# Ten and four extra products on TensorE around the state's part of two pieces, in a kernel of a chunked scan and two dense layers

## The chip, the core and the metric

The kernel runs on one core of a Trainium2 chip. That core has five engines that work side by side and wait for each other through semaphores: PE (TensorE, the matrix products, with PEld for its weight loads), DVE (VectorE), ACT (ScalarE), POOL (GpSimd) and SP (SyncE, which here only issues transfers). Each engine takes its own instructions in a fixed order. The metric is the time of one execution of the whole program, in microseconds of device time; the median of several runs counts.

## The reference, cut to what matters

```python
log_a = np.log(np.clip(a, 1e-06, 1.0))
for c in range(nc):                                  # 24 chunks of 32 steps
    cum = np.cumsum(la, axis=-1)
    M = np.einsum('bhin,bhjn->bhij', Cc, Bc) * np.exp(cum_i - cum_j) * causal
    y[:, :, sl] = M @ xc + (Cc @ state) * np.exp(cum)
    state = decay_full * state + sum_j(Bc_j xc_j * decay_from_j)
x = y.transpose(0, 2, 1, 3).reshape(3072, 256)
g = lrelu(x @ w_in)            # 256 -> 2048, slope 0.01
x = g @ w_out                  # 2048 -> 256
h = relu(x @ w2_in)            # 256 -> 2048
out = (h * h) @ w2_out         # 2048 -> 256
```

A scan over 4 sequences of 768 steps (8 heads, head size 32, state size 16) gives 3072 rows of 256 numbers. Two dense layers follow, each 256 to 2048 to 256, with a leaky relu in the first and a squared relu in the second. All of it is wanted in fp32.

## The kernel before, in words

**Tiling.** The 3072 rows are cut into 12 *pieces* of 256 steps (TP), three to a sequence. The scan of a piece (scan_piece, L300) writes the piece's rows as a pair yh and yl (L389, L390): an upper part that TensorE can take as fp32r, and the rest. The pieces are gathered into 8 *blocks*: the first four blocks are one piece each, the last four two pieces each. A block goes through layer 1 and then through layer 2. The constant ORDER (L39) says in which order: "10 11 12 20 ..." is layer 1 of blocks 0, 1 and 2, then layer 2 of block 0, and so on. I write "block 11" for layer 1 of block 1, as ORDER does; blocks 10, 11 and 12 need pieces 0, 1 and 2.

**A layer of a block.** The 2048 middle columns are 16 tiles of 128. For a block of one piece two tiles make a *group*, so a layer has eight groups. A group has 12 first products (hmm, L417 to L419, into a PSUM tile hp of the pool ph, which has three buffers under one tag "h"), its activation (act: gh and t on ACT, gl on DVE at L433), and 12 second products (omm: eight with gh at L445 and L446, four with gl at L450), which add up over all groups in two PSUM tiles o0 and o1. When the last group is in, finish (L452) copies o out: upper part on ACT (L458), lower part yl on DVE (L459). Each of o0 and o1 has one buffer only, so the next layer's second products wait for these copies.

**A piece's scan.** TensorE has three short bursts: 32 products S (L340, L341), 48 products Y (L365 to L367), and at the end 32 products that add the earlier state's part to Y (L385, L386). Between the last two lies the state's chain: the scan stt on DVE (L212), its split in two parts shl (ACT L374, DVE L376), the transpose t16 on DVE (L378), four transfers into the block-diagonal operand sbd (L310), and the 32 products; then ACT writes yh (L389) and DVE yl (L390), and the block's first hmm can start.

**Weights.** They arrive as 64-bit words and are taken apart in the kernel: load_w issues the transfer, split_w (ACT L129, L132), split_w1 (DVE L140, L141) and split_w2 (ACT L152, DVE L153) make an upper and a lower part of each of the 32 chunks. All of it happens in the first 150 us, beside the scans.

**What sets the order.** The code emits scan steps, weight steps and groups interleaved; a scheduler then fixes the order of each engine's instructions before the program runs. On the chip an engine does not leave that order: what stands behind a waiting instruction waits too.

Of the kernel before, what the change touches and what calls it, by code (L numbers as in the profile page):

```python
# [8 lines left out]
F32 = mybir.dt.float32  # L9
# [9 lines left out]
P = 128  # L19
# [18 lines left out]

ORDER = "10 11 12 20 13 21 14 22 23 15 24 16 25 17 26 27"  # L39
LAG = {1: 2, 2: 3}  # L40
W_AHEAD = 4


@with_exitstack
def ssd_moe_kernel(ctx: ExitStack, tc: tile.TileContext, in1, in2, w1i, w1o, w2i, w2o, out):
# [6 lines left out]
    nc = tc.nc  # L52
# [7 lines left out]
    ph = ctx.enter_context(tc.tile_pool(name="ph", bufs=3, space=bass.MemoryType.PSUM))  # L60
# [14 lines left out]
    xbh = cp.tile([P, U, 4, T], F16, name="xbh")  # L75
# [14 lines left out]
    w_hi, w_lo = {}, {}  # L90
# [19 lines left out]
    def load_w():  # L110
        nm, c = wq.pop(0)
        if nm == "2o" and c >= 5:
            st = yp.tile([P, 2, 256], I64, tag="y2", name="wst")
        else:
            st = wp.tile([P, 2, 256], I64, tag="w", name="wst")
        if nm[1] == "i":
            sl = (slice(None), slice(None), slice(c * 256, c * 256 + 256))
        else:
            sl = (slice(None), slice(2 * c, 2 * c + 2), slice(None))
        nc.sync.dma_start(st, w_dram[nm][sl])  # L120
        w_loaded.append((nm, c, sl, st))
# [50 lines left out]
    def load_piece(p):  # L172
        v = sp.tile([P, U * (N + T + D)], F32, tag="in1", name="in1")
        w = sp.tile([P, U * 2 * T], F32, tag="in2", name="in2")
        nc.sync.dma_start(v, in1[p])
        nc.sync.dma_start(w, in2[p])
        return part(v, N + T, D), part(v, 0, N), part(w, T, T), part(v, N, T), part(w, 0, T), part(w, 0, T + N)
# [38 lines left out]
    def in_chunks(v):  # L216
        return v.rearrange("p k (c t) -> p (k c) t", t=T)
# [59 lines left out]
    def powers(mx):  # L277
# [19 lines left out]
        nc.vector.tensor_tensor(sbp, sc[:, 2:3], pm, ALU.mult)  # L297
        return sc, isc, sbp

    def scan_piece(p, tiles, get_y):  # L300
        x_t, b_t, bt_t, ct_t, az, mk = tiles
        if p < NPC:
# [60 lines left out]
        for u in range(U):  # L363
            o = Y[:, u, 0 : T + N]
# [8 lines left out]
        shl = sp.tile([P, HG, NC, 2, N], F16, tag="xh", name="shl")  # L373
        nc.scalar.copy(shl[:, :, :, 0, :], sv)  # L374
        yield
        nc.vector.tensor_tensor(shl[:, :, :, 1, :], sv, shl[:, :, :, 0, :], ALU.subtract)  # L376
        t16 = sp.tile([P, U, D], F16, tag="xl", name="t16")
        nc.vector.transpose(t16.rearrange(fl), shl.rearrange("p g c k n -> p (g c k n)"))  # L378
        yield
# [3 lines left out]
        for u in range(U):  # L383
            o = Y[:, u, 0:T]
            nc.tensor.matmul(o, sbd[:, u], qh[:, u], start=False, stop=False, skip_group_check=True)  # L385
            nc.tensor.matmul(o, sbd[:, u], ql[:, u], start=False, stop=True, skip_group_check=True)  # L386
        yield
        yh, yl = (in_chunks(v) for v in get_y())
        nc.scalar.activation(yh, Y[:, :, 0:T], AF.Copy, scale=fac)  # L389
        nc.vector.scalar_tensor_tensor(yl, Y[:, :, 0:T], fac, yh.bitcast(F32), ALU.mult, ALU.subtract)  # L390


# [96 lines left out]
    loaded = {0: load_piece(0)}  # L489
    for _ in range(W_AHEAD):  # L490
        load_w()

    def scans():
        for p in range(NP):
            bd = sequence_scales(p // NPC + 1) if p % NPC == NPC - 1 and p + 1 < NP else iter(())
            for i, _ in enumerate(scan_piece(p, loaded.pop(p), piece_y(p))):
                if i == QN[p] - 7 and p + 1 < NP:
                    loaded[p + 1] = load_piece(p + 1)
                next(bd, None)
                yield p  # L500
            for _ in bd:
                pass
            yield p
# [29 lines left out]
    def second(lag):  # L533
        while len(pend) > lag:
            ph_, ms = pend.pop(0)
            ph_.omm(ms)
            if ms[-1] == KO - 1:
                ph_.finish()
# [3 lines left out]
    for layer, i in order:  # L542
        p0, n = blocks[i]
        yh, yl = ys.pop(i) if layer == 2 else ys[i]
        ph_ = Phase(layer, p0, n, yh, yl)
        for m in range(0, KO, 2 // n):
# [7 lines left out]
            pend.append((ph_, ms))  # L554
            second(LAG[n])
            acc += 1.0 if len(wq) > 18 else 0.4
# [55 lines left out]
```

## Time and profile before

| | |
|---|---|
| median of 3 runs | 652.35 us (650.02 to 653.43) |
| the profiled execution | 649.59 us |
| its span, first to last instruction | 647.8 us |
| PE busy in the span | 592.5 us, 91% |
| DVE busy in the span | 420.4 us, 65% |
| ACT busy in the span | 356.9 us, 55% |
| mean granted TensorE clock | 0.989 |

The busy shares are means over stages with different limits. "Granted clock" is the share of TensorE's full clock: 1.00 is 2.4 GHz, 0.50 is 1.2 GHz, and anything between is a mix of the two within the stretch that is shown. An instruction's listed duration is longer than the step to the next one of its kind, because instructions overlap at their ends; what a row of instructions costs is the distance between their starts.

### The profile page before, as it was taken

How to read it: one execution, taken by the hardware profiler on the slowest of the kernel's cores; microseconds unless marked ns; L12 is line 12 of the kernel's file. 1: busy time of each engine (PE TensorE's matmuls, PEld its weight loads, DVE VectorE, ACT ScalarE, POOL GpSimd, SP SyncE). 2: the span in 40 equal slices, each digit the busy share in tenths (PEclk: the TensorE clock that was granted, in tenths of full speed). 3: DMA queues.
4: the chain of work that ended last, by engine and by line, in shares of the span. 5: the costliest groups of instructions: out<-in, count | busy, mean ns of one | idle time of the engine just before them, and what ended most of it. 6: DMA issues, size and time to landing. Idle time of an engine off the chain costs nothing.

```text
span 647.8 us, 11305 instructions
## 1 busy us (share of the span) xinstructions
PE 592.5 (91%) x4440; PEld 514.8 (79%) x4440; DVE 420.4 (65%) x726; ACT 356.9 (55%) x630; POOL 5.1 (1%) x14
## 2 busy tenths in 40 slices
PE   0278695999999999999999999999999999999997
PEld 0177595999999988899987888888888888788885
DVE  7989999898768854576554586563565322554553
ACT  5999776665555545545535555455544433544442
POOL 3000000000000000000000000000000000000000
PEclk9999898899999999999999999999999999999999
DMA  9775765423635422202212212212000000000000
GB/s 323 240 242 136 238 138 150 127 61 65 172 33 149 76 73 24 50 34 42 50 50 25 50 33 25 50 66 25 8 1 10 33 0 1 0 1 2 32 2 32
DMA packets 111397, 46.48 MB, mean 72 GB/s; under 512 B 94320, under 2 KB 101104, under 8 KB 111344
## 3 DMA queue, kind: packets, MB, share of 16 engines
q1 hardware_dynamic: 111344, 45.76, 27.2%
q8 instruction: 35, 0.57, 0.4%
q14 instruction: 18, 0.15, 0.1%
HBM read 36.83 MB, written 3.15 MB: 62 GB/s over the span
## 4 chain that ended last, share of the span: by engine, by line
PE 72%; DVE 16%; ACT 4%; DMA 4%; issue 3%; SPq 0%; DVEq 0%; ACTq 0%
PE o L445 12%; PE hp L417 12%; PE hp L419 12%; PE hp L418 11%; PE o L446 11%; PE o L450 11%; DMA all<-in 3%; DVE gl L433 2%; DVE wst L140 2%; DVE wst L141 2%; DVE t L431 1%; DVE mx L266 1%; DVE e L194 1%; DVE lt L188 1%; DVE wl1i L153 1%
## 5 line engine op out<-in xcount | busy, mean ns | idle before, releaser
L433 DVE TENSOR_TENSOR gl<-t,gh 128x512 fp32r<-128x512 f32 x192 | 132.0, 688 | 130.1 <-ACT t L428 80.4
L427 ACT ACTIVATE gh<-hp 128x512 fp32r<-128x512 f32 x96 | 57.2, 596 | 95.4 <-PE o L446 77.8
L432 ACT CAST gh<-t 128x512 fp32r<-128x512 f32 x96 | 59.6, 621 | 74.8 <-DVE t L431 64.5
L417 PE MATMUL hp<-yl,wh1i 128*128 128x256 f32 (+1 forms) x256 | 89.4, 349 | 9.5 <-DVE yl L390 9.5
L431 DVE TENSOR_TENSOR t<-t 128x512 f32<-128x512 f32 x96 | 66.1, 688 | 44.5 <-ACT t L430 44.4
L418 PE MATMUL hp<-yh,wh1i 128*128 128x256 f32 (+1 forms) x256 | 88.8, 347 | 0.0
L419 PE MATMUL hp<-yh,wl1i 128*128 128x256 f32 (+1 forms) x256 | 88.8, 347 | 0.0
L430 ACT ACTIVATE t<-hp 128x512 f32<-128x512 f32 x96 | 57.3, 597 | 57.2 <-PE hp L419 54.6
L445 PE MATMUL o<-gh,wl1o 128*128 128x256 f32 (+1 forms) x256 | 84.8, 347 | 3.6 <-DVE wl1o L153 3.4
L417 PE MATMUL hp<-yl,wh2i 128*128 128x256 f32 (+1 forms) x256 | 86.8, 339 | 0.0
L419 PE MATMUL hp<-yh,wl2i 128*128 128x256 f32 (+1 forms) x256 | 86.5, 338 | 0.0
L418 PE MATMUL hp<-yh,wh2i 128*128 128x256 f32 (+1 forms) x256 | 86.2, 337 | 0.0
L445 PE MATMUL o<-gh,w2o 128*128 128x256 f32 (+1 forms) x256 | 83.6, 343 | 2.1 <-DVE yl L459 1.9
L446 PE MATMUL o<-gh,wh1o 128*128 128x256 f32 (+1 forms) x256 | 82.8, 339 | 0.0
L446 PE MATMUL o<-gh,w2o 128*128 128x256 f32 (+1 forms) x256 | 81.7, 336 | 0.0
L417 PEld LDWEIGHTS hp<-yl,wh1i 128*128 128x128 f32 x256 | 50.7, 198 | 15.1 <-issue 5.8
L450 PE MATMUL o<-gl,wh1o 128*128 128x256 f32 (+1 forms) x256 | 61.1, 339 | 0.6 <-DVE gl L433 0.6
L450 PE MATMUL o<-gl,w2o 128*128 128x256 f32 (+1 forms) x256 | 60.8, 337 | 0.0
L445 PEld LDWEIGHTS o<-gh,wl1o 128*128 128x128 f32 x256 | 48.2, 188 | 12.0 <-DVE wl1o L153 5.8
L428 ACT ACTIVATE t<-hp 128x512 f32<-128x512 f32 x96 | 56.9, 593 | 0.0
L419 PEld LDWEIGHTS hp<-yh,wl1i 128*128 128x128 f32 x256 | 50.6, 198 | 5.9 <-issue 0.2
L418 PEld LDWEIGHTS hp<-yh,wh1i 128*128 128x128 f32 x256 | 50.8, 198 | 5.4
(124 smaller groups left out, 982.1 us busy)
## 6 DMA issues: line engine op xcount, KB each, us to landing
in<-in SPq DMA_DIRECT2D x12, 640.0 KB, 4.5
in<-in SPq DMA_DIRECT2D x12, 512.0 KB, 3.3
all<-in SPq DMA_DIRECT2D x15, 384.0 KB, 3.7
wst<-w1i SPq DMA_DIRECT2D x8, 512.0 KB, 9.2
wst<-w1o SPq DMA_DIRECT2D x8, 512.0 KB, 4.6
wst<-w2o SPq DMA_DIRECT2D x8, 512.0 KB, 5.7
wst<-w2i SPq DMA_DIRECT2D x8, 512.0 KB, 5.0
out_t<-ob SPq DMA_DIRECT2D x8, 256.0 KB, 2.2
```

The source lines that it names most:

```text
L417: nc.tensor.matmul(hp, wh, self.xl[:, :, k], start=(k == 0), stop=False)
L418: nc.tensor.matmul(hp, wh, self.xh[:, :, k], start=False, stop=False)
L419: nc.tensor.matmul(hp, wl, self.xh[:, :, k], start=False, stop=(k == KI - 1))
L427: nc.scalar.activation(gh, hp, AF.Lrelu)
L428: nc.scalar.activation(t, hp, AF.Lrelu)
L430: nc.scalar.activation(t, hp, AF.Relu)
L431: nc.vector.tensor_tensor(t, t, t, ALU.mult)
L432: nc.scalar.copy(gh, t)
L433: nc.vector.tensor_tensor(gl, t, gh.bitcast(F32), ALU.subtract)
L445: nc.tensor.matmul(self.o[d], wl, gh, start=(m == 0), stop=False)
L446: nc.tensor.matmul(self.o[d], wh, gh, start=False, stop=False)
L450: nc.tensor.matmul(self.o[d], wh, gl, start=False, stop=(m == KO - 1))
```

## The change

A helper warm(a, b, n) takes a PSUM tile of the pool ph under the tag "h", the same three buffers that hold hp, and runs n products of 512 columns into it. Nobody reads that tile. It is called twice in the scan of pieces 1 and 2: ten products right after DVE has written the lower part of shl (their moving operand is shl, their stationary operand the first slice of xbh), and four products right after ACT has written yh (moving operand yh, stationary operand the first weights of layer 1). Nothing else is edited. Line numbers move by up to 12.

```diff
--- before.py
+++ after.py
@@ -38,6 +38,7 @@
 
 ORDER = "10 11 12 20 13 21 14 22 23 15 24 16 25 17 26 27"
 LAG = {1: 2, 2: 3}
+WARM = (1, 2)
 W_AHEAD = 4
 
 
@@ -297,6 +298,12 @@
         nc.vector.tensor_tensor(sbp, sc[:, 2:3], pm, ALU.mult)
         return sc, isc, sbp
 
+    def warm(a, b, n):
+
+        o = ph.tile([P, 512], F32, tag="h", name="warm")
+        for _ in range(n):
+            nc.tensor.matmul(o, a, b, start=True, stop=True)
+
     def scan_piece(p, tiles, get_y):
         x_t, b_t, bt_t, ct_t, az, mk = tiles
         if p < NPC:
@@ -374,6 +381,8 @@
         nc.scalar.copy(shl[:, :, :, 0, :], sv)
         yield
         nc.vector.tensor_tensor(shl[:, :, :, 1, :], sv, shl[:, :, :, 0, :], ALU.subtract)
+        if p in WARM:
+            warm(xbh[:, 0].rearrange("p h t -> p (h t)"), shl.rearrange("p g c k n -> p (g c k n)"), 10)
         t16 = sp.tile([P, U, D], F16, tag="xl", name="t16")
         nc.vector.transpose(t16.rearrange(fl), shl.rearrange("p g c k n -> p (g c k n)"))
         yield
@@ -385,8 +394,11 @@
             nc.tensor.matmul(o, sbd[:, u], qh[:, u], start=False, stop=False, skip_group_check=True)
             nc.tensor.matmul(o, sbd[:, u], ql[:, u], start=False, stop=True, skip_group_check=True)
         yield
-        yh, yl = (in_chunks(v) for v in get_y())
+        ya = get_y()
+        yh, yl = (in_chunks(v) for v in ya)
         nc.scalar.activation(yh, Y[:, :, 0:T], AF.Copy, scale=fac)
+        if p in WARM:
+            warm(w_hi["1i"][:, 0, 0:P], ya[0].rearrange("p k t -> p (k t)"), 4)
         nc.vector.scalar_tensor_tensor(yl, Y[:, :, 0:T], fac, yh.bitcast(F32), ALU.mult, ALU.subtract)
```

The scheduler orders the whole program anew. DVE's order is the same as before up to its row 127, and the same again for its last 305 rows; PE's is the same for its first 325 rows and its last 4306. In between the rows are reordered. Three places are shown.

PE, the third piece (piece 2): the end of the state's products (Y from sbd) and what follows. hp_1464 is the first group of block 12, which reads piece 2's yl_1401 and yh_1400. Before:

```order
L385 MATMUL Y_1233<-qh_1185,sbd_96 128x32
L386 LDWEIGHTS sbd_96
L386 MATMUL Y_1233<-ql_1186,sbd_96 128x32
L417 MATMUL hp_1464<-yl_1401,wh1i_110 128x256
L418 MATMUL hp_1464<-yh_1400,wh1i_110 128x256
L419 MATMUL hp_1464<-yh_1400,wl1i_111 128x256
L417 MATMUL hp_1464<-yl_1401,wh1i_110 128x256
L418 MATMUL hp_1464<-yh_1400,wh1i_110 128x256
```

In the changed kernel piece 2's pair is called yl_1428 and yh_1427, and yl_338 and yh_337 is the pair of the two blocks before:

```order
L395 MATMUL Y_1249<-ql_1202,sbd_96 128x32
L305 MATMUL warm_1430<-yh_1427,wh1i_110 128x512 x4
L429 MATMUL hp_1456<-yl_338,wh1i_110 128x256
L430 MATMUL hp_1456<-yh_337,wh1i_110 128x256
L431 MATMUL hp_1456<-yh_337,wl1i_111 128x256
L429 MATMUL hp_1456<-yl_338,wh1i_110 128x256
L430 MATMUL hp_1456<-yh_337,wh1i_110 128x256
L431 MATMUL hp_1456<-yh_337,wl1i_111 128x256
L429 MATMUL hp_1456<-yl_338,wh1i_110 128x256
L430 MATMUL hp_1456<-yh_337,wh1i_110 128x256
L431 MATMUL hp_1456<-yh_337,wl1i_111 128x256
L429 MATMUL hp_1456<-yl_338,wh1i_110 128x256
```

The four extra products wait for yh_1427, and the last group of block 11 (12 first products, hp_1456) now stands behind them; its 12 second products come later still. Before, all of block 11 stood ahead of the state's products. At the second piece it is alike: the last group of block 10 stands behind the four products, and the last but one behind the ten.

DVE, the stretch that ends with the third piece's yl (yl_1401). yl_338 from o0_1148 and o1_1149 is the finish of block 11. Before:

```order
L153 TENSOR_TENSOR wl2i_115<-wst_812,wh2i_114 128x2x256
L459 TENSOR_TENSOR yl_338<-o0_1148,yh_337 128x256
L459 TENSOR_TENSOR yl_338<-o1_1149,yh_337 128x256
L140 SCALAR_TENSOR_TENSOR wst_885<-wst_885 128x512
L194 SCALAR_TENSOR_TENSOR e1_1567<-in2_1286,d1e_97 128x512
L141 SCALAR_TENSOR_TENSOR wst_885<-wst_885 128x512
L342 TENSOR_TENSOR e1_1567<-in1_1285,e1_1567 128x512
L333 SCALAR_TENSOR_TENSOR xl_1603<-in1_1285,sc_1190,xh_1490 128x512
L153 TENSOR_TENSOR wl2i_115<-wst_885,wh2i_114 128x2x256
L140 SCALAR_TENSOR_TENSOR wst_940<-wst_940 128x512
L323 SCALAR_TENSOR_TENSOR kmx_1483<-in2_1286,sc_1190,him_1443 128x512
L390 SCALAR_TENSOR_TENSOR yl_1401<-Y_1233,fac_984,yh_1400 128x512
```

In the changed kernel piece 2's lower part, yl_1428, stands two rows above the first of these; yl_338 from o0_1164 and o1_1165 is the finish of block 11:

```order
L154 TENSOR_TENSOR wl2i_115<-wst_1087,wh2i_114 128x2x256
L141 SCALAR_TENSOR_TENSOR wst_1323<-wst_1323 128x512
L141 SCALAR_TENSOR_TENSOR wst_1454<-wst_1454 128x512
L142 SCALAR_TENSOR_TENSOR wst_1323<-wst_1323 128x512
L445 TENSOR_TENSOR gl_1471<-t_1469,gh_1470 128x512
L142 SCALAR_TENSOR_TENSOR wst_1454<-wst_1454 128x512
L445 TENSOR_TENSOR gl_1511<-t_1509,gh_1510 128x512
L154 TENSOR_TENSOR w2o_1900<-wst_1323,w2o_1900 128x512
L367 SCALAR_TENSOR_TENSOR ql_1788<-e1_1599,sc_1206,qh_1787 128x512
L445 TENSOR_TENSOR gl_1551<-t_1549,gh_1550 128x512
L471 TENSOR_TENSOR yl_338<-o0_1164,yh_337 128x256
L471 TENSOR_TENSOR yl_338<-o1_1165,yh_337 128x256
```

The finish of block 11 moved from ahead of piece 2's yl to 12 rows behind it, and weight steps (wst, wl2i) that stood behind yl now stand ahead of it.

DVE, the finish of block 12 (yl_1401 from o0_1570 and o1_1571), which is followed by layer 2 of block 0. Before:

```order
L141 SCALAR_TENSOR_TENSOR wst_1917<-wst_1917 128x512
L459 TENSOR_TENSOR yl_1401<-o0_1570,yh_1400 128x256
L433 TENSOR_TENSOR gl_1934<-t_1932,gh_1933 128x512
L459 TENSOR_TENSOR yl_1401<-o1_1571,yh_1400 128x256
L153 TENSOR_TENSOR w2o_2199<-wst_1917,w2o_2199 128x512
L431 TENSOR_TENSOR t_1981<-t_1981 128x512
L194 SCALAR_TENSOR_TENSOR e1_2272<-in2_1942,d1e_97 128x512
L333 SCALAR_TENSOR_TENSOR xl_2306<-in1_1941,sc_1190,xh_2238 128x512
L433 TENSOR_TENSOR gl_1983<-t_1981,gh_1982 128x512
L431 TENSOR_TENSOR t_2024<-t_2024 128x512
L342 TENSOR_TENSOR e1_2272<-in1_1941,e1_2272 128x512
L266 TENSOR_REDUCE mx_2661<-all_2662 128x1
```

In the changed kernel (yl_1428 from o0_1602 and o1_1603):

```order
L141 SCALAR_TENSOR_TENSOR wst_1949<-wst_1949 128x512
L383 TENSOR_TENSOR shl_2020<-stt_1971,shl_2020 128x16x16
L142 SCALAR_TENSOR_TENSOR wst_1949<-wst_1949 128x512
L387 STREAM_TRANSPOSE t16_2064<-shl_2020 128x512
L443 TENSOR_TENSOR t_1922<-t_1922 128x512
L154 TENSOR_TENSOR w2o_2231<-wst_1949,w2o_2231 128x512
L349 TENSOR_TENSOR e1_2304<-in1_1973,e1_2304 128x512
L445 TENSOR_TENSOR gl_1924<-t_1922,gh_1923 128x512
L267 TENSOR_REDUCE mx_2693<-all_2711 128x1
L443 TENSOR_TENSOR t_1964<-t_1964 128x512
L471 TENSOR_TENSOR yl_1428<-o0_1602,yh_1427 128x256
L471 TENSOR_TENSOR yl_1428<-o1_1603,yh_1427 128x256
```

The row e1<-in1 and a reduction mx<-all, which stood behind the finish, stand ahead of it now, and so do the scan e1 and another mx<-all, a few rows above the piece shown.

## Rows read from the trace of the kernel before

**Rows 1.** The page's head.

```profile
span 647.8 us, 11305 instructions
```

**Rows 2.** Stretches: length, busy us (instructions) of each engine, granted clock, DMA.

```profile
core 0: us, PE busy (x) PEld busy (x) DVE busy (x) ACT busy (x) POOL busy (x), PEclk, DMA share, GB/s
60.00:147.00 87.00, 70.35 (x747) 67.44 (x745) 83.39 (x162) 62.32 (x116) 0.00 (x0) 0.92 0.54 151
75.00:85.00 10.00, 8.40 (x58) 8.31 (x58) 9.73 (x28) 8.93 (x18) 0.00 (x0) 0.83 0.71 224
105.00:110.00 5.00, 1.11 (x34) 0.89 (x32) 5.00 (x8) 3.29 (x8) 0.00 (x0) 0.84 0.44 46
115.00:120.00 5.00, 5.00 (x31) 5.00 (x30) 3.61 (x8) 2.44 (x5) 0.00 (x0) 0.64 0.51 60
147.00:648.00 501.00, 494.90 (x3396) 422.22 (x3396) 282.51 (x445) 243.40 (x427) 0.00 (x0) 1.00 0.18 39
```

**Rows 3.** PE in order of time, second piece: start, length, engine, line, operation.

```profile
76.78 0.39 PE L417 MATMUL hp<-yl,wh1i 128*128 128x256 f32 x1 [1.60 <-DVE yl L390]
...
77.77 0.42 PE L418 MATMUL hp<-yh,wh1i 128*128 128x256 f32 x1
...
80.97 0.33 PE L418 MATMUL hp<-yh,wh1i 128*128 128x256 f32 x1
81.14 0.28 PE L419 MATMUL hp<-yh,wl1i 128*128 128x256 f32 x1
81.26 0.27 PE L417 MATMUL hp<-yl,wh1i 128*128 128x256 f32 x1
```

**Rows 4.** PE in order of time, third piece; in brackets the idle time before.

```profile
107.60 0.18 PE L385 MATMUL Y<-qh,sbd 128*128 128x32 f16 x1 [2.46 <-DMA sbd<-t]
...
114.29 0.55 PE L417 MATMUL hp<-yl,wh1i 128*128 128x256 f32 x1 [5.72 <-DVE yl L390]
114.64 0.42 PE L418 MATMUL hp<-yh,wh1i 128*128 128x256 f32 x1
...
118.48 0.35 PE L418 MATMUL hp<-yh,wh1i 128*128 128x256 f32 x1
```

**Rows 5.** ACT and DVE in order of time, ahead of the third piece's first products.

```profile
111.33 0.67 ACT L389 ACTIVATE yh<-Y,fac 128x512 fp32r<-128x512 f32 x1
112.73 0.75 DVE L323 SCALAR_TENSOR_TENSOR kmx<-in,sc,him 128x512 f16<-128x512 f32 x1
113.40 0.74 DVE L390 SCALAR_TENSOR_TENSOR yl<-Y,fac,yh 128x512 fp32r<-128x512 f32 x1
```

**Rows 6.** DVE's waits, 60 to 147 us: in total, times, longest.

```profile
DVE gl L433 <- ACT t L428: 1.8, 3, 1.4
DVE mx L266 <- DMA all<-in: 1.0, 2, 0.7
```

**Rows 7.** DVE in order of time: distances between starts.

```profile
62.28 0.69 DVE L140 SCALAR_TENSOR_TENSOR wst<-wst 128x512 int32<-128x512 int32 x1
62.88 0.69 DVE L433 TENSOR_TENSOR gl<-t,gh 128x512 fp32r<-128x512 f32 x1
...
78.64 1.22 DVE L194 TENSOR_TENSOR_SCAN e<-in,d1e 128x512 f32<-128x512 f32 x1
79.78 0.93 DVE L266 TENSOR_REDUCE mx<-all 128x1 f32<-128x768 f32 x1
80.62 0.14 DVE L243 TENSOR_SCALAR er<-rb 128x1 int32<-128x1 int32 x1
...
107.06 0.74 DVE L459 TENSOR_TENSOR yl<-o,yh 128x256 fp32r<-128x256 f32 x2
```

**Rows 8.** All engines in order of time, where block 12 ends and layer 2 begins.

```profile
146.57 0.41 DVE L459 TENSOR_TENSOR yl<-o,yh 128x256 fp32r<-128x256 f32 x1
...
147.04 0.39 PE L445 MATMUL o<-gh,w2o 128*128 128x256 f32 x1 [1.30 <-DVE yl L459]
...
147.50 0.41 DVE L459 TENSOR_TENSOR yl<-o,yh 128x256 fp32r<-128x256 f32 x1
```

**Rows 9.** PE's waits, 148 to 648 us: in total, times, longest.

```profile
PE Y L385 <- DMA sbd<-t: 0.7, 1, 0.7
PE o L445 <- DVE yl L459: 0.6, 1, 0.6
PE S L286 <- DVE dg L284: 0.3, 1, 0.3
```

## The prediction

> **What bounds the kernel now.** I read the page's head first [rows 1]: the span is 647.8 us, and the profiled execution took 649.59, so 1.8 us lie around it. The median of the runs shown is 652.35, 2.76 us more; I make the sum against 649.59 and add 2.76 at the end.
>
> Then I read the busy times by stage [rows 2], because the page's 91% for PE is a mean over two different stages. From 147 us on PE is busy 494.90 of 501 us at the full clock: there the end is set by how much PE still has to do, and a microsecond lost ahead of it is a microsecond at the end. From 60 to 147 us it is otherwise: DVE is busy 83.39 of 87 us, PE 70.35. Whether PE's gaps in that stage can close depends on what stands in DVE's queue.
>
> Then PE's rows around the two pieces. At the second piece the first products wait 1.60 us for yl and start at full clock, one every 0.12 us; from the start at 77.77 to that at 80.97 there are 15 steps of 0.213 us, and from 81.14 on 0.12 again [rows 3]. At the third piece PE waits 2.46 us for the transfers into sbd, runs the 32 products, and then stands idle for 5.72 us until DVE has written yl [rows 4]; the granted clock falls to half meanwhile (0.84 over 105 to 110 us, 0.64 over 115 to 120) [rows 2], and from 114.64 to 118.48 there are 18 steps of 0.213 [rows 4]. These slow stretches are what the extra products can act on.
>
> Last, the two releasers. yh is done at 112.00, but yl starts only at 113.40, right behind kmx: DVE has no gap there, it comes to yl when its queue does [rows 5]. And at 147.04, where layer 2 of block 0 begins its second products, PE has waited 1.30 us for the finish of block 12 on DVE [rows 8]. So DVE's queue sets both points at which PE waits longest.
>
> **The change, part by part.**
>
> *The clock.* If it stays full, 15 steps shrink from 0.213 to 0.12 at the second piece: 15 x 0.094 = 1.4 us, with the two steps at the ends 1.5. At the third piece 18 x 0.094 = 1.7, with the first and last step 1.9. Together 3.4 us of PE time; the lower bound is nothing, if the clock falls all the same.
>
> *The products themselves.* No row shows one of 512 columns in this stage. Two steps of 256 columns at full clock make 0.24 us [rows 3], at half clock 0.43. Ten cost 2.4 (4.3) us and four 0.95 (1.7) for each piece. The ten wait for DVE's lower part of shl, and the groups behind them wait as well; the cover is the idle time that followed in any case (2.46 us and 5.72 us [rows 4]). The four lie between yh and yl: yh at 112.00 plus 0.95 is 112.95, and PE was idle until 114.29. So none of the 28 lies on the path, as long as yl comes no earlier. Uncovered, all 28 would cost 6.7 us.
>
> *The group that moved behind the four products.* At the third piece PE has 24 more products to do after yh than before, the last group of block 11. Its 12 first products (1.4 us) take 112.95 to 114.4, which is when yl was ready. Its 12 second products, 1.4 us, are new work behind yl. Against the 1.9 us of the clock that leaves PE 0.5 us ahead. At the second piece the same happens, but PE's 5.72 us of idle time at the third swallow whatever it brings there.
>
> *A wait that gets longer.* The 32 products with sbd now stand on PE behind the second products of block 11's seventh group, whose gl (gl_1391) DVE does ten rows after the transpose. By DVE's steps (below) that is 6 us after it, near 110 us, and puts these products at about 110.2 instead of 107.60. yh follows near 111.9. DVE comes to yl at 113.4, so 1.5 us of cover is left and the cost is nothing; without the cover it would be what exceeds 1.5.
>
> *DVE's queue, the term that decides.* I counted the rows ahead of two points, before and after, and priced each by the distance between starts [rows 7]: 0.60 for a weight step, gl or a plain 512-column operation, 1.14 for the scan e1, 0.84 for a reduction mx<-all, 0.37 for one copy yl<-o. Ahead of the third piece's yl there are three wst rows and one wl2i more (+2.4), one gl (-0.6) and two copies (-0.74) fewer: +1.1 us. Ahead of the finish of block 12 there are one scan e1 (+1.14), one plain row e1<-in1 (+0.6), one w2o row (+0.6) and two reductions (+1.68) more: +4.0 us. That is the upper bound of how much later DVE comes to this finish, for which PE already waits [rows 8].
>
> The lower bound is set by DVE's idle time, which can fill up: 87 less 83.39, so 3.6 us from 60 to 147 [rows 2], of which 1.8 is gl waiting for ACT behind block 12's slow first products and 1.0 the reductions waiting for their transfers [rows 6]. If all of it closes, DVE comes 0.4 us later. I take the gl waits as closed (a whole group more of gl work is at hand, and block 12's products come fast) and most of the waits of the reductions: 2.5 of 3.6, nearer the full recovery, since the rows on which those waits rest move apart. That leaves +1.5 us at 147.04. PE itself would be there 0.5 us earlier than before, so it waits longer, and it is DVE's 1.5 us that pass on.
>
> *Behind it.* From 148 us on PE has 1.6 us of waits left: 0.7 for sbd, 0.6 for a finish, 0.3 for dg [rows 9]. The chains behind the first and the last do not hang on PE, so part of them closes when PE is late; I take 0.5, between nothing and 1.0.
>
> The sum: +1.5 - 0.5 = +1.0 us, so 650.6 against the profile's 649.59, and **653.4 us** beside the median of 652.35. That is 0.16%; about 0.5%, or 3.3 us, is what a measurement of this kernel can tell from no change.
>
> The Trainium skill (page "Perfetto Trace Analysis", sections "Identifying the Most-Contended Engine" and "Optimization Strategy") says to work on the engine with the highest occupancy, and that this engine may be another one in each regime of a kernel. Taken over the whole page, the rule names PE (91%) and would give the clock's 3.4 us in full; taken over 60 to 147 us, it names DVE and gives the sum above. The row of the stage is the nearer one, and I follow it.
>
> **The rivals.**
>
> *The clock's gain passes through.* If PE, not DVE, sets the time through the stage, all 3.4 us arrive: 652.35 - 3.4 = 649.0. For it speaks that over 115 to 120 us PE is busy all the time and DVE only 3.61 of 5 us [rows 2]. Against it, that at both ends of this stretch it waited for DVE, and that DVE has more to do in front of both. It decides if DVE comes to block 12's finish no later than before, that is if it recovers over 4.0 us where it has 3.6 to recover. Chance 0.12. The Trainium skill (page "TensorE: Matmul & The Clock Gate", section "Why this matters for your kernels") advises to leave no idle gaps between bursts of products, so that the full clock lasts. By that alone the time would be this rival's; the rows on the clock agree with the rule, those on DVE say that its gain has no way to the end.
>
> *DVE recovers nothing.* The second reduction that moved ahead of block 12's finish needs a transfer that can only be issued when the first one is read. If DVE waits there as it did before for such transfers (0.7 us at the longest [rows 6]), or its other waits only move, the whole +4.0 arrives and nothing closes behind: 656.4. It decides if DVE's idle time between 60 and 147 us is still 3.6 us or more. For it speaks that some 240 rows of DVE's order are new, so that a wait that closes at one row can open at another. Chance 0.17.
>
> *The change doesn't do what it says.* The clock falls at the third piece all the same: ahead of the four products PE still has idle time, before and after the 32 small products. The four then take 1.7 us to 113.7 and the 12 first products 2.6 to 116.3; the slow stretch, as long as before, ends at about 116.2. PE is then 2.0 us late for block 12 less 1.9 for starting it at full clock, and with the group's second products 1.5 us late. It had 1.30 us to wait at 147.04 [rows 8] and now has DVE's 1.5 us more: the time is the same 653.4, with at most 0.5 on top. Chance 0.23.
>
> **How the numbers follow.** My own sum has 0.48. The prediction is 653.4. Within 0.5% of 652.35 lie 0.45 of my sum's 0.48, 0.20 of the fallen clock's 0.23, 0.05 of the first rival's 0.12 (649.0 is just at the bound) and 0.06 of the second's 0.17: 0.76. Faster by over 0.5%: 0.07 from the first rival and 0.02 from the two sums: 0.09. Slower: 0.11 from the second and 0.04 from the two sums: 0.15. The range goes from 649.5, which leaves out most of the first rival, to 656.5, the upper bound of DVE's term; below it lie some 0.09, above it some 0.09.
>
> **What would show it.** The clock: granted clock of 1.00 over 75 to 85 us and about 115 to 120, steps of 0.12 us in block 12's first products. The cover: no idle time of PE closed by the extra products alone, and yl of the third piece within 1.5 us of 114.1. DVE: idle time of about 1 us from 60 to 147 in place of 3.6. The finish of block 12: PE's wait for yl L459 (L471 then) at least as long as 1.30 us, its end near 148.5. From there to the end the distance should be that of before, 500.8 us (647.8 less 147.04), shorter by no more than 1.0.
>
> I am wrong if PE waits for nothing near 147 us: then something else than DVE set the pace, and the time is lower. And I am wrong if DVE meets a new wait of over 2 us, on a transfer or on PE's reordered groups, ahead of block 12's finish: then it is higher.

## The result, and the profile after

The changed kernel takes **654.75 us** (median of 8 runs, 653.73 to 656.60) beside 651.83 us for the kernel before (8 runs, 649.72 to 653.43): ratio 1.006, 95% interval 1.0044 to 1.0075. The medians lie 2.9 us apart; the ratio, which is not that of the medians, stands for 3.9 us. Forecast were 653.4 beside 652.35, which is 1.0 us slower. The time lies in the range, the sign is right, and the loss is three to four times the forecast one.

The profiled execution of the change took 656.38 us, with a span of 654.6. Its stretches, columns as in [rows 2]:

```profile
60.00:147.00 87.00, 75.39 (x786) 69.45 (x786) 84.40 (x162) 62.70 (x113) 0.00 (x0) 1.00 0.56 154
75.00:85.00 10.00, 8.25 (x62) 7.79 (x63) 8.53 (x21) 6.64 (x12) 0.00 (x0) 1.00 0.90 298
105.00:110.00 5.00, 3.74 (x22) 2.44 (x21) 5.00 (x10) 3.19 (x7) 0.00 (x0) 1.00 0.62 139
115.00:120.00 5.00, 4.70 (x35) 4.52 (x36) 5.00 (x9) 3.34 (x7) 0.00 (x0) 1.00 0.38 39
147.00:655.00 508.00, 499.21 (x3412) 426.53 (x3410) 282.35 (x446) 244.57 (x431) 0.00 (x0) 0.99 0.18 38
```

The granted clock is 1.00 where it was 0.83, 0.84 and 0.64, and over 60 to 147 us 1.00 in place of 0.92. But it is 0.99 behind 147 us, where it was 1.00. PE around the two pieces, in order of time, answering to [rows 3, 4]:

```profile
75.74 1.19 PE L305 MATMUL warm<-yh,wh1i 128*128 128x512 f32 x4 [0.34 <-ACT yh L399]
76.76 0.28 PE L429 MATMUL hp<-yl,wh1i 128*128 128x256 f32 x1
76.89 0.28 PE L430 MATMUL hp<-yh,wh1i 128*128 128x256 f32 x1
...
105.50 2.32 PE L305 MATMUL warm<-shl,xbh 128*128 128x512 f16 x10 [1.69 <-DVE shl L383]
107.47 0.47 PE L429 MATMUL hp<-yl,wh1i 128*128 128x256 f32 x1
...
112.40 0.73 PE L462 MATMUL o<-gl,wh1o 128*128 128x256 f32 x4 [1.13 <-DVE gl L445]
112.97 0.19 PE L394 MATMUL Y<-qh,sbd 128*128 128x32 f16 x1
...
115.30 1.20 PE L305 MATMUL warm<-yh,wh1i 128*128 128x512 f32 x4 [1.36 <-ACT yh L399]
116.34 0.28 PE L429 MATMUL hp<-yl,wh1i 128*128 128x256 f32 x1
116.46 0.27 PE L430 MATMUL hp<-yh,wh1i 128*128 128x256 f32 x1
```

All first products of 256 columns run one every 0.12 us; the 15 and 18 steps of 0.213 us are gone. The idle 5.72 us of [rows 4] is gone too. What came in its place stands where block 12 ends and layer 2 begins (DVE's finish and PE's first o with w2o, answering to [rows 8]), and right behind it:

```profile
150.06 0.76 DVE L471 TENSOR_TENSOR yl<-o,yh 128x256 fp32r<-128x256 f32 x2
...
150.55 0.39 PE L457 MATMUL o<-gh,w2o 128*128 128x256 f32 x1 [1.69 <-DVE yl L471]
...
151.58 0.41 PE L458 MATMUL o<-gh,w2o 128*128 128x256 f32 x1
151.80 1.05 PE L462 MATMUL o<-gl,w2o 128*128 128x256 f32 x4
152.65 0.41 PE L429 MATMUL hp<-yl,wh2i 128*128 128x256 f32 x1
152.86 0.41 PE L430 MATMUL hp<-yh,wh2i 128*128 128x256 f32 x1
...
154.78 0.37 PE L430 MATMUL hp<-yh,wh2i 128*128 128x256 f32 x1
154.99 0.28 PE L431 MATMUL hp<-yh,wl2i 128*128 128x256 f32 x1
155.11 0.29 PE L457 MATMUL o<-gh,w2o 128*128 128x256 f32 x1
```

PE waits 1.69 us where it waited 1.30, and 1.0 us after the wait its products take 0.213 us each again, until 154.99. PE's waits behind 147 us (in total, times, longest) were 0.7, 0.6 and 0.3 in [rows 9] behind the one at 147.04; now there is, besides the 1.7 just shown, one for the state's transfers, and another slow stretch follows it:

```profile
PE Y L394 <- DMA sbd<-t: 2.5, 1, 2.5
PE o L457 <- DVE yl L471: 1.7, 1, 1.7
```

Read alone, this pair of profiles says: 3.5 us lost up to block 12's finish, 3.3 behind it. It is 6.8 us apart where the medians are 2.9 apart, so I profiled both kernels once more before reading on.

### The profile page after: what moved, and what is told of

Same layout as the page of the kernel before. It is cut to its first block, busy times and chain, and to the rows that moved or that the text cites. A ratio compares the mean times of both kernels' runs of the same rounds, so it can differ in the third digit from the quotient of the medians.

```text
span 654.6 us, 11368 instructions
## 1 busy us (share of the span) xinstructions
PE 599.8 (92%) x4468; PEld 519.0 (79%) x4468; DVE 420.3 (64%) x726; ACT 357.6 (55%) x630; POOL 5.1 (1%) x14
## 4 chain that ended last, share of the span: by engine, by line
PE 79%; DVE 13%; ACT 3%; DMA 3%; issue 2%; SPq 0%; DVEq 0%; ACTq 0%
PE o L457 13%; PE hp L429 12%; PE o L462 12%; PE hp L431 12%; PE hp L430 12%; PE o L458 12%; DVE wst L142 2%; DMA in<-in 1%; DVE gl L445 1%; DVE wst L141 1%; DVE e L195 1%; DVE lt L189 1%; DMA all<-in 1%; DVE wl1i L154 1%; PE Y L394 1%
## 5 line engine op out<-in xcount | busy, mean ns | idle before, releaser
L457 PEld LDWEIGHTS o<-gh,w2o 128*128 128x128 f32 x256 | 48.0, 188 | 8.3 <-DVE yl L471 2.1
```

The costliest lines, as they stand in the source:

```text
L457: nc.tensor.matmul(self.o[d], wl, gh, start=(m == 0), stop=False)
```

## Experiments

**Both kernels a second time** (no edit).

Kernel before: 

> The kernel before, profiled once more. In the first piece, which the change leaves alone, the 0.213 us steps of block 10's first products end at 40.0 us in the profile of before and at 42.3 in that of the change. If this end differs from one execution to the next, it lies elsewhere here, and block 12's finish (147.04 us) moves with it, by 1 to 2 us. If it is fixed by the program, it is at 40.0 again and the finish at 147.0.

The change: 

> The changed kernel, profiled once more. If the end of the first piece's slow steps differs from one execution to the next, the clock behind 147 us does as well: the slow stretches at 151.6 and 193.1 us are then gone or elsewhere, and the span is 1 to 3 us under 654.6. If they belong to the changed order, both are there again, and so is the wait of 2.5 us for the transfers into sbd near 192 us.

Measured: 652.53 and 652.17 us; the *slower* one of these two is the kernel before. The four profiles side by side ("finish" is the start of PE's first o<-gh,w2o; the second column is where the first piece's steps of 0.213 us end, which this change does not touch):

| | first piece's slow steps end | finish | finish to end of span |
|---|---|---|---|
| before, 1st profile | 40.0 | 147.04 | 500.8 |
| before, 2nd | 42.5 | 149.66 | 501.1 |
| change, 1st | 42.3 | 150.55 | 504.0 |
| change, 2nd | 40.0 | 148.16 | 502.2 |

So part of what the first pair showed was the executions', not the change's. I call an execution early when these steps end at about 40 us, and late when they end at about 42.5. DVE waits for S of that piece (row m<-S: 0.8 us in the early executions, 1.8 in the late ones). That makes 1.0 of the 2.6 us between the two finishes of the kernel before. Most of the rest enters at one reduction, which waits longer for its transfer in the late execution; the kernel before, early and late:

```profile
84.22 0.95 DVE L266 TENSOR_REDUCE mx<-all 128x1 f32<-128x768 f32 x1 [0.27 <-DMA all<-in]
87.37 0.95 DVE L266 TENSOR_REDUCE mx<-all 128x1 f32<-128x768 f32 x1 [1.71 <-DMA all<-in]
```

The change waits at such a reduction for 1.23 us in its late execution (79.49) and not at all in its early one (76.94). Whether the longer wait follows from the first piece's delay is not shown. Early beside early and late beside late, the finish comes 1.1 and 0.9 us later with the change, and the way from there to the end is 1.5 and 2.9 us longer: means 1.0 and 2.2, in sum 3.2 beside the medians' 2.9. The stretches of the second profiles, before above, the change below:

```profile
60.00:147.00 87.00, 70.42 (x738) 67.49 (x738) 82.03 (x159) 61.87 (x114) 0.00 (x0) 0.90 0.55 150
147.00:160.00 13.00, 11.70 (x122) 11.41 (x121) 11.17 (x18) 7.56 (x15) 0.00 (x0) 1.00 0.35 55
```

```profile
60.00:147.00 87.00, 76.96 (x799) 71.01 (x798) 85.69 (x164) 63.66 (x116) 0.00 (x0) 1.00 0.56 154
147.00:160.00 13.00, 11.84 (x110) 11.77 (x111) 8.31 (x14) 5.36 (x9) 0.00 (x0) 0.87 0.38 63
```

DVE's idle time from 60 to 147 us is 3.6 and 5.0 us before, 2.6 and 1.3 with the change: 2.3 us are recovered. And the clock falls behind the finish in both profiles of the change (0.87 over 147 to 160 us; the first profile's row reads the same 0.87) and in neither of before (1.00). The second slow stretch, near 193 us, is in the first profile only.

One limit holds for all that follows: the scheduler orders each edited kernel anew. I give the number of DVE's 726 rows that would have to move to make two orders equal (names without buffer numbers, so it is a lower bound). Between the kernel before and the change it is 62; change and order alone, 35; ten alone and the ten's place, 66; the two lighter kernels, 58 of 694; before and first piece alone, 3; change and the change with the next gap filled, none. Only there does an edit add products and change nothing else.

**The order without the products.**

```diff
-        for _ in range(n):
-            nc.tensor.matmul(o, a, b, start=True, stop=True)
+        nc.tensor.matmul(o[:, 0:32], a, b[:, 0:32], start=True, stop=True)
```

> Each call of the helper here makes one product of 32 columns instead of ten or four of 512: the tile is allocated and the order of all engines is nearly that of the change (the last groups stand behind the extra products, DVE has the same rows ahead of block 12's finish), but nothing fills PE's gaps. Theory A (the order costs time, by DVE's 2 to 4 us more of work ahead of block 12's finish): as slow as the change, ratio to before 1.004 to 1.008, with the clock falling at both pieces as before. Theory B (the products themselves cost, the order does not): like before, ratio 0.998 to 1.002. Theory C (the products' full clock is worth its 3.4 us, and the order costs more than the change shows): slower than the change, ratio 1.009 to 1.012.

Measured: ratio 1.0031 (1.0017 to 1.0044), 2.1 us slower. An order of this kind costs time without the products. The ratio lies between the ranges of A (from 1.004) and B (to 1.002), and its interval touches both; C, by which this kernel had to be slower than the change, falls. Beside the change's 2.9 us (3.9 by the ratio), the 28 products, with all they do for the clock, come out at +0.9 us (1.9) and not at a gain. The early profiles show two sides of that. The finish is at 150.12 in an early execution (40.2), 3.1 us later than in the early one of before and 2.0 later than in that of the change (148.16): up to the finish the products earn. Behind it this kernel needs 500.3 us and the change 502.2: there it is lost again.

**The products without a turn among hp's buffers.**

```diff
-        o = ph.tile([P, 512], F32, tag="h", name="warm")
+        o = pz.tile([P, U, T], F32, tag="S", name="warm").rearrange(fl)
```

> The extra products write a tile of the pool pz under the tag S instead of one of the three buffers that hold hp. So they take no turn among the groups, and PE's groups stand where they stood before: 96 and 192 first products ahead of the state's products of the second and third piece, none moved behind the four. By the prices of the rows DVE has 2.4 us more ahead of block 12's finish than before (the change: the same). Theory A (DVE's work ahead of that finish decides): ratio 1.002 to 1.006. Theory C (PE's clock decides once the groups stay): ratio 0.995 to 0.998. If the turn among hp's buffers is the whole cost: 0.998 to 1.002.

Measured: ratio 1.0037 (1.0023 to 1.0050). All groups stand ahead of the state's products again, and it is still 2.1 us slower: a loss of this size does not need the moved groups. The size agrees with A. The clock is not held at the third piece here (0.56 over 115 to 120 us), though all 28 products run.

**The ten alone, the four alone** (the other call is left out).

Ten alone: 

> Only the ten products behind shl, none behind yh. No group moves behind the state's products, and DVE has 0.3 us more than before ahead of block 12's finish. Theory A (order): like before, ratio 0.998 to 1.002. Theory B (the products cost): ten products at 0.24 us on two pieces, up to 4.8 us in part uncovered, ratio 1.002 to 1.007. The clock should still fall in the gap ahead of the third piece's yl, since nothing fills it.

Four alone: 

> Only the four products behind yh, none behind shl. The last group of blocks 10 and 11 moves behind them as in the change, and DVE has 1.6 us more than before ahead of block 12's finish. Theory A (order): ratio 1.002 to 1.005, most of the change's loss. Theory B (the products cost, and the ten are most of them): ratio 0.998 to 1.002.

Measured: ten alone 1.0068 (1.0048 to 1.0087), four alone 1.0003 (0.9990 to 1.0016). Both are against A: by the prices of DVE's rows the four should have cost most and the ten nothing. The ten cost 4.5 us when alone, in B's range.

**The ten's place with one small product** (the edit of the order alone, made to the kernel with the ten alone).

> As the kernel with the ten products alone (ratio 1.0068), but each of its two calls makes one product of 32 columns: the tile keeps its turn among hp's three buffers, and by the prices of the rows DVE has 0.6 us less than before ahead of block 12's finish. Theory G (the tile's turn, and the order that follows from it, cost the most): ratio 1.003 to 1.006. Theory H (the ten products' own 2.3 us on PE at each piece cost the most): ratio 0.998 to 1.002.

Measured: **0.9969** (0.9954 to 0.9983), 1.9 us *faster* than before. Against the ten alone that is 6.4 us for ten real products at two pieces, more than the 2 x 1.97 us from their first start to that of the next product (105.50 to 107.47 above). The tile's turn does not cost by itself, so G falls; the time lies even below H's range (from 0.998). That the products make the whole 6.4 us is not shown, because 66 of DVE's rows stand elsewhere in the two kernels.

**Less work for DVE.** The second of DVE's two operations on each 64-bit weight word is left out, from the kernel before and from the change; some bits of the weights are then missing.

```diff
-        nc.vector.scalar_tensor_tensor(w0, w1, -(1 << 31), w0, ALU.bitwise_and, ALU.bitwise_or)
```

Before, lighter: 

> The kernel before without the second of DVE's two operations on each 64-bit word of the weights (some bits of the weights are then missing from the output's products): by the prices of the rows DVE has 17 us less to do ahead of block 12's finish. Theory A (DVE is the bound up to 147 us): faster than before by 5 to 12 us, ratio 0.981 to 0.992. If DVE is not the bound there: 0.996 to 1.000.

Change, lighter: 

> The change without the same operation of DVE. Theory A (the full clock is worth 3.4 us of PE, and DVE's queue hides it): with DVE's queue shorter the change pays, 1 to 3.4 us less than the lighter kernel before, a quotient of the two ratios of 0.995 to 0.998. Theory D (the ten products push the work behind them back on PE, whatever DVE has to do): 1 to 4 us more, a quotient of 1.002 to 1.006.

Measured: 0.9871 (0.9845 to 0.9897) and 0.9909 (0.9881 to 0.9936): 643.08 and 645.20 us. DVE does bound the stage, since less of it takes 7.6 us off the kernel before. But with DVE busy only 74.2 and 74.3 of the 87 us, the change still costs 2.1 us. The clock was held better in five of the six executions of the lighter change (0.994 to 0.996 over the span, against 0.987), though not in the one profiled (0.988). That DVE's queue *hides a gain* of the clock has no support here: with the queue shorter no gain appears. The time is the one D expected. The lighter kernels are ordered anew as well, so the 2.1 us can't be put to one row, nor to the products alone.

**The next gap filled as well.** Four more products, into the tile of layer 2's third group, ahead of that group's own:

```diff
+FILL_M, FILL_N = 4, 4
...
+            if self.layer == 2 and self.t0 == 0 and ms[0] == FILL_M:
+                for _ in range(FILL_N):
+                    nc.tensor.matmul(self.h, w_hi["2i"][:, 0, 0:P], self.xh.rearrange("p a k t -> p (a k t)"), start=True, stop=True)
```

> The change, with four more unread products of 512 columns on PE just ahead of the first products of layer 2 of block 0's third group, that is in the place where PE waits for block 12's finish (1.68 and 1.69 us in the two profiles of the change); DVE's and PE's order is otherwise that of the change. They need no wait and take 0.95 us of the idle time. Theory E (behind 147 us the change loses 1.0 to 1.6 us because the clock falls after this wait): no steps of 0.213 us between 148 and 156 us, ratio to before 1.002 to 1.005. Rival (the clock falls there for another reason, or its fall costs nothing in the end): ratio 1.005 to 1.008 as the change, or the slow steps are still there.

Measured: 1.0039 (1.0023 to 1.0055), 1.4 us better than the change's 1.0060 by the middle values; the intervals overlap. PE around the finish, in order of time:

```profile
148.51 1.09 PE L427 MATMUL hp<-yh,wh2i 128*128 128x512 f32 x4
149.45 0.28 PE L433 MATMUL hp<-yl,wh2i 128*128 128x256 f32 x1
...
151.77 0.39 PE L461 MATMUL o<-gh,w2o 128*128 128x256 f32 x1 [0.74 <-DVE yl L475]
...
152.92 0.64 PE L466 MATMUL o<-gl,w2o 128*128 128x256 f32 x4
153.40 0.28 PE L433 MATMUL hp<-yl,wh2i 128*128 128x256 f32 x1
```

The wait is 0.74 us and the steps behind it are 0.12: the four hold the clock there, as E says. This profile has a slow stretch further on, behind a wait of 1.99 us at 191.4 (granted clock 0.79 over 190 to 198 us). One execution of this kernel had a mean granted clock of 1.000 over its span and took 653.58 us, and executions of the change with 0.997 and 0.998 took 653.73 to 654.80, while the kernel before, at 0.982 to 0.989, has its median at 651.4. So an execution can be some 2 us slower with hardly any slow clock. But these are single executions, of which it is not known if they were early or late, and the early and the late one of before are 2.9 us apart; they don't settle how much of the loss is the clock's.

**The first piece.** Seven products behind its shl and four behind its yh (with yh as both operands, since the weights are not there yet), alone; and together with the four of the second and third piece:

```diff
-WARM = (1, 2)
+WARM = {0: (7, 4)}
...
+WARM = {0: (7, 4), 1: (0, 4), 2: (0, 4)}
```

The two calls take their numbers of products from this table (their edit is not shown).

Alone: 

> Extra products for the first piece alone: seven behind shl and four behind yh; the order of all other instructions is that of before on PE and on DVE. Theory F (the first piece's slow steps, 14 of 0.213 us in one profile of before and 25 in the other, pass on to DVE through its wait for S, 0.8 and 1.8 us, and through DVE's queue to the end): fewer slow steps at 37 us, DVE's wait for S under 0.5 us, ratio 0.995 to 0.998. Rival (DVE's time there is idle time that closes later): 0.999 to 1.001. If seven and four products don't hold the clock: steps of 0.213 us still there, 0.999 to 1.001.

With the four: 

> Seven and four products for the first piece, and the four behind yh for the second and third (the ten there left out). If the first piece's gain (0.8 to 1.8 us) adds to the four's result (ratio 1.0003): 0.996 to 0.999. If the reordering that the four bring takes it back: 0.999 to 1.002.

Measured: **0.9975** (0.9961 to 0.9989) and 0.9999 (0.9979 to 1.0019). In the first piece the products lie in idle time of PE (3.35 us ahead of the seven; only the four end 0.5 us late in the first kernel's profile), the order stays nearly as it was (3 rows of DVE and 11 of PE would have to move, not none as expected), and the slow steps fall from 14 and 25 to 7 in the profile of the first kernel and none in that of the second. The gain, 1.1 us by the medians and 1.6 by the ratio, has the size that F forecast. F's path for it is not shown: DVE's longest wait for S in the first kernel's profile is 0.8 us still, against the 0.5 expected, and its finish is at 148.36, later than the early 147.04 of before. Whether the four on top take the gain back is open: by the ratio they do, by the medians (650.12 and 650.22 us) not, and three of the twelve executions took 653.5 to 655.0 us where the others took 651.0 at most.

The profiles in one table (one execution each; "slow stretches" counts the stretches of 0.213 us steps behind the finish, and "busy" is PE's busy time from the finish to the end):

| | ratio | wait at the finish | slow stretches | finish to end | busy |
|---|---|---|---|---|---|
| before (two profiles) | 1 | 1.30, 1.30 | 0, 0 | 500.8, 501.1 | 494.9, 494.9 |
| change (two profiles) | 1.0060 | 1.69, 1.68 | 2, 1 | 504.0, 502.2 | 497.3, 496.0 |
| tile in S | 1.0037 | 1.84 | 1 | 501.4 | 495.8 |
| ten alone | 1.0068 | 1.95 | 2 | 505.7 | 497.9 |
| change and next gap filled | 1.0039 | 0.74 | 1 | 502.0 | 495.8 |
| order alone | 1.0031 | 1.75 | 0 | 500.3 | 494.6 |
| four alone | 1.0003 | 1.55 | 0 | 500.4 | 494.6 |
| ten's place, one product | 0.9969 | 1.37 | 0 | 500.5 | 494.6 |
| first piece alone | 0.9975 | 1.30 | 0 | 501.6 | 495.1 |
| first piece and the four | 0.9999 | 1.59 | 0 | 499.7 | 494.4 |
| lighter before | 0.9871 | 1.44 | 1 | 502.6 | 496.2 |
| lighter change | 0.9909 | 2.37 | 1 | 501.1 | 495.7 |

PE's products behind the finish are the same in number in all of them, but for one or two that some orders put ahead. Its busy time there follows the slow stretches: 494.4 to 495.1 us with none, 495.7 to 496.2 with one, 497.3 and 497.9 with two. The rest of the column before it is idle time. All six profiles with the ten real products have a slow stretch behind the finish; of the eight without them, only the lighter kernel before has one. From the finish to the end, kernels with the ten take 501.4 to 505.7 us and kernels without them 499.7 to 501.6; the lighter pair does not fit this, with 501.1 and 502.6.

## Why the prediction was right in sign and short in size

*The clock at the two pieces* was right: 1.00 in both profiles, no steps of 0.213 in block 11's and block 12's first products. The rival by which it falls all the same is not excluded in every execution: the profile with the next gap filled, whose order is that of the change, has 0.78 over 105 to 120 us.

*DVE's queue* was right in mechanism and nearly in size, once executions of a kind are compared: of DVE's idle time 2.3 us were recovered (2.5 taken), and the finish comes 1.0 us later (1.5 taken). The order alone fits the term as well: there the clock falls (0.51 over 105 to 110 us, 0.66 over 115 to 120) and the finish comes 2.0 us later than with the change, where I had counted 1.8 for the waits that close when block 12's products come fast. The first pair of profiles alone would have said 1.0 recovered and 3.5 later. That PE waits at the finish at least 1.30 us came true, with 1.69 and 1.68. The rows' prices, however, don't rank the variants: four alone has 1.6 us more ahead of the finish and loses nothing that can be measured, ten alone has 0.3 more and loses 4.5. And what follows from this term, that the clock's 3.4 us would come through if DVE had less to do, found no support in the lighter kernels.

*The products themselves*, taken as nothing on the path, failed for the ten, as far as the runs tell the products from the order. I priced them about right (2.4 us; 1.97 by their starts) and let them hide in idle time that followed. At the piece itself that is how it went: the state's products start at 110.59 in the early execution (110.2 forecast), and yl of the third piece at 113.60 and 115.99, against 113.40 and 116.28 before (1.1 us later by the rows' prices). Yet between the ten alone and their place with one small product lie 6.4 us, partly a new order of DVE's rows (0.9 us by their prices). By the profiles the loss shows behind the finish (505.7 against 500.5 us), not at the piece: the finishes, 149.97 in a late execution and 147.56 in an early one, lie no further apart than those of before. Of these 5.2 us 3.3 are PE's busy time, with two slow stretches against none, and 1.9 its idle time, 1.7 of it a longer wait for the state's transfers (2.60 us at 192.2, against 0.93). How the ten bring this about so far behind them is open; no run moved the ten within the piece, and none kept the order.

*Behind it* is the step that failed most: I let 0.5 us of the delay be absorbed behind 147 us, and bounded it by nothing and 1.0. It is 2.2 us *longer* instead (1.5 and 2.9). I had read from [rows 9] that PE has few waits there, and from [rows 2] that it has the full clock, and took both as given. Of the 2.2 us 1.8 are PE's busy time (1.1 and 2.4), which is the slow stretches, and 0.4 its idle time. In both profiles of the change the clock falls behind the longer wait at the finish: some 16 steps of 0.213 for 0.12, 1.5 us. In one it falls again near 193 us, behind a wait of 2.5 us of the state's products (1.24 in the other; 0.74 and 1.16 in the two of before). This second wait can be followed back, here in the first profile of the change (SP's queue issuing piece 4's input, DVE's first row with it, PE's state products):

```profile
177.81 0.34 SPq L177 DMA_DIRECT2D in<-in  x1
...
182.86 0.18 DVE L185 TENSOR_SCALAR d1e<-in 128x16 f32<-128x16 f32 x1 [3.62 <-DMA in<-in]
...
192.25 0.18 PE L394 MATMUL Y<-qh,sbd 128*128 128x32 f16 x1 [2.50 <-DMA sbd<-t]
```

and in the kernel before:

```profile
173.36 0.34 SPq L176 DMA_DIRECT2D in<-in  x1
...
176.64 0.19 DVE L184 TENSOR_SCALAR d1e<-in 128x16 f32<-128x16 f32 x1 [1.59 <-DMA in<-in]
...
186.00 0.19 PE L385 MATMUL Y<-qh,sbd 128*128 128x32 f16 x1 [0.74 <-DMA sbd<-t]
```

Counted from the finish, and with the second profiles behind the first: the input is issued at 27.3 and 26.8 us (26.3 and 26.3 before), DVE's row starts at 32.3 and 31.0 (29.6 and 30.1), PE's products at 41.7 and 40.4 (39.0 and 39.4). By these times a delay behind the finish reaches the next input, and that chain comes back to PE; no run tests this link by itself. The waits behind the finish sum to 2.50 and 2.02 us, against 1.62 and 1.92 before.

The filled gap supports the first half of this (no fall, 1.4 us less by the middle values, not separated by the intervals). What it doesn't explain: the kernel with the order alone waits 1.75 us at the finish and keeps its clock, and the lighter kernel before, with no extra product at all, waits 1.44 us and loses it (its steps are 0.213 until 143.65, from a finish at 138.65). So neither the length of the wait nor the ten products decide it alone; what does is open.

So the sign has the reason forecast for it, but that reason makes 1.0 of the 3.2 us by which the profiles differ. That the time still lies in the range is luck as far as the part behind the finish goes: +2.2 us stand there in place of -0.5, and the range, made wide for DVE's term, had room for it.

## What to carry to other kernels

Filling an engine's idle time to keep a clock is worth what the stage's bound lets through, and it moves the next gap: look for the first wait behind the filled stretch, and price its growth and what the clock does there, before counting steps saved. Products that nobody reads paid here where PE was idle ahead of them and the order of the rest stayed nearly the same, in the first piece (0.9975); where other groups stood behind them they cost nothing that can be measured (the four, 1.0003) or 4.5 us (the ten). Ask also if the edit changes the order of the rest: where it does, the difference is not that of the products alone. And compare executions of a kind: one profile of each kernel was off by more than the change.

## What was not expected of the hardware

The same instructions, ahead of any edit, ran at two speeds for different lengths of time: PE's steps in the first piece went from 0.213 to 0.12 us at 40.0 in one execution and at 42.5 in another of the same kernel, 14 and 25 slow steps. The Trainium skill (page "TensorE: Matmul & The Clock Gate", section "Part 1: The HAM clock gate (the "warmup" mystery)") says that the number of slow products differs from run to run of one kernel, and the traces agree. Beside a change of 2.9 us it is not small: the two finishes lie 2.6 us apart, of which DVE's wait behind these steps makes 1.0, and the times 2.9 (649.59 and 652.53). In that stretch the view of the granted clock does not show the slow steps; kernel before, first profile, 36 to 40 us and, for comparison, 147 to 160:

```profile
36.00:40.00 4.00, 3.36 (x15) 3.36 (x16) 3.79 (x7) 3.54 (x7) 0.00 (x0) 1.00 0.92 308
147.00:160.00 13.00, 12.96 (x132) 12.87 (x133) 10.24 (x16) 6.68 (x12) 0.00 (x0) 1.00 0.28 48
```

That is no half speed at a full clock. The trace's first record of the clock is the rise itself, at 40.11 us here and at 42.47 in the second profile, where the slow steps end; ahead of it the view has no record and shows 1.00. The mean granted clock of an execution does not count these steps either.

And small changes of order alone move this kernel by as much as the change does: one product of 32 columns per piece in a tile that takes its turn among hp's buffers made it 1.9 us faster, two such tiles per piece 2.1 us slower.
